# GFNet mixing and SwiGLU block: the order of loads and weight conversion in the first batch's head

## The chip, the cores and the metric

The kernel runs on one core of one Trainium2 chip. That core has TensorE (PE, with its weight loads PEld), VectorE (DVE), ScalarE (ACT), GpSimd (POOL) and SyncE (SP), and 16 DMA engines that serve the transfers which SP, ACT and POOL issue. The metric is the device time of one execution in microseconds. A profiled execution gives a span, which is a little shorter than the device time of the same execution.

## The reference

Eight batches of 3008 tokens with 256 channels are mixed along the tokens by a real Fourier transform, a multiplication with a complex filter and the inverse transform. Then every token passes a SwiGLU block with 1536 hidden channels. All values are float32 on the way in and out; the weights of the block come as 64-bit floats.

```python
X = np.fft.rfft(x, axis=1)
F = (filt_r + 1j * filt_i)[None, :, :]
y = np.fft.irfft(X * F, n=x.shape[1], axis=1)      # (8, 3008, 256)
x = y.reshape(8 * 3008, 256)
g = x @ w_gate                                     # (24064, 1536)
silu = g * (1.0 / (1.0 + np.exp(-g)))
out = (silu * (x @ w_val)) @ w_out                 # (24064, 256)
```

## The kernel before

**The whole.** The transform of length 3008 is split as 47 x 64. Batch by batch, a class `Spectral` carries it out in steps, and a class `Group` does the SwiGLU part. A batch has 8 chunks of tokens and the hidden layer has 3 parts, so 24 group steps make one batch. While TensorE works on the groups of batch b, the transform of batch b+1 is placed between them by a list of tokens (`SCHEDULE`). Only the first batch's transform has nothing to hide behind. It is the head of the program, and this case is about it. Every instruction of the head is issued by `pin`, which keeps the order in which the Python code issues it, so the order on each engine's queue is the order of the code. Each engine works its queue strictly in that order, and an instruction that waits holds everything behind it on that engine.

**The head's steps.** Four pieces of x (about 0.77 MB each) are loaded by `Spectral.load_x` into space that is lent by other tiles. `stage1_first(u)`, u = 0 to 7, is the first short transform: TensorE multiplies (L844), and the result is copied out of PSUM by ACT for one half of the channels and by DVE for the other (both L848). `turn(u)`, u = 0 to 11, transposes a unit on TensorE (L857), and ACT copies it (L861). `stage2a(u)`, u = 0 to 11, multiplies a unit by a table `tb` (L871). DVE then multiplies by the filter `f` in three operations of some 0.7 us (L880 with the filter's real part for both halves of the rows, L884 and L887 with the imaginary part), and POOL adds the two products (L326; for the last unit DVE does it). The real part is wanted in both halves of the rows, so `real_part(u)` copies it twice (L897): by POOL for every third unit (0, 3, 6, 9), else by ACT. `stage2b(u)`, four units behind, multiplies back by the table (L904), ACT copies the result (L912, the last one in two pieces L910), and it is written to DRAM (tensor `d`, L915). Units 0 to 7 are written from SP's queue, 8 to 11 from ACT's. `load_tables(i)`, i = 0 to 5, loads the table and the filter for two units: one transfer of 512 KB and four of 128 KB.

**Reload and stage 3.** `load_t4(0, i, part)` reloads the written result (`f<-d`), first the rows of units 0 to 7, then those of units 8 to 11. `stage3(0, step)` is the last transform for chunk 0 (L941). After it the first group begins (L1035). In front of stage 3 stand matmuls on zeros and on weights that compute nothing that is kept (`idle`, L578): five on zeros, one on the weights from slot A13 on and one on those from slot A01 on. The last two wait for those weights.

**The weights.** The 64-bit weights are turned into float32 on the chip, by halves of 262 KB. `weight_halves()` lists them: 8 hidden halves and 8 output halves for each of the 3 parts. `load_weights(i)` loads half i. `round_half(i)` converts it in nine small pieces: DVE takes the bits apart (L403, L406), ACT makes the power of two (L408, L411, L413, L415), DVE puts sign and low bits in (L418, L422), and POOL multiplies and adds up (L442, L443, then L329 or L326; L430 for an output half). Buffers for these are few: a half i uses the buffer of an earlier half, so its first operation on DVE waits until POOL has finished with that one. `combine_weights(g, i, j)` makes sums of converted halves for a pair of blocks: an add on DVE (L326 or L333), for some pairs a scaling on ACT (L464), a subtraction on POOL (L329), and an add on DVE for the first four pairs of part 0 and on POOL for the others.

**The ticks.** The class `Preparation` holds a timetable: to each tick belongs a list of such pieces. Half i starts four ticks after half i-1, half 8 (the first output half) eight ticks after half 7, and the pieces of a half stand at 0, 1, 2, 3, 4, 6, 7, 9 and 10 ticks from its start. The six pairs of part 0 are combined from tick 39 on. `tick(step, n)` issues the pieces of the next n ticks. With `hold=True` the pieces on POOL are kept back until `release()`. `finish(step)` issues all ticks that must stand before a group step. During the groups of batch 0, 20 ticks are issued per group step.

**The order in the code.** In the head, SP loads the four pieces of x, and then weight halves and tables in turn. Four ticks are issued at stage 1's last step, two after the first turns, two in each of the first ten units of stage 2a, and one in each of the last three rounds of stage 2b. `finish(0)` then issues the rest, 16 ticks, before stage 3.

Of the kernel before, what the change touches and what calls it, by code (L numbers as in the profile page):

```python
# [71 lines left out]
N_TWO = NS // NV  # L72
# [30 lines left out]
BLOCKS = (0, 1, 3, 2)  # L103
# [100 lines left out]
def kernel(  # L204
# [165 lines left out]
    def spot_of(i):  # L370

        spot = (i - N_EARLY) % 5
        return spot if i < N_LENT and spot < 3 else None
# [3 lines left out]
    def load_weights(i):  # L377
        if i in raws or i >= len(weights):
            return
        if i < N_EARLY:  # L380
            raws[i] = early_raw(i)
        elif spot_of(i) is not None:
            raws[i] = bits(4 * 7 * 128 + 512 * spot_of(i))
        else:
            raws[i] = rpool.tile([128, 2, 128, 2], U32, name=f"raw_{i}", tag="raw", bufs=2)
        pin(nc.sync.dma_start(out=raws[i], in_=weights[i][0]))
# [65 lines left out]
    def combine_weights(g, i, j):  # L452

        d = j - i
        wt_f = weights_of(0, 0, g).rearrange("p s z f -> p s (z f)")
        m = wt_f[:, SLOT[f"A{i}{j}"]]
        ui, uj, yi, yj = [wt_f[:, SLOT[f"{p}{q}"]] for p in "PQ" for q in (i, j)]
        if d == 1:
            pin(negated_sum(m, ui, uj))
        else:  # L460
            pin(add(nc.vector, m, ui, uj))
        yield
        if d > 1:
            pin(nc.scalar.mul(m, m, -1.0 / d))  # L464
        yield
        pin(sub(nc.gpsimd, wt_f[:, SLOT[f"B{i}{j}"]], yi, m))
        early = g == 0 and PAIRS_USED.index((i, j)) < 4
        pin(add(nc.vector if early else nc.gpsimd, wt_f[:, SLOT[f"E{i}{j}"]], yj, m))
# [10 lines left out]
    class Preparation:  # L479
# [3 lines left out]
        def __init__(self):  # L483
            self.at, self.held = 0, []

            self.ticks, self.need = {}, {}
            base, ready = [], {}

            def put(t, f, by, pool=False):
                self.ticks.setdefault(t, ([], []))[pool].append(f)  # L490
                self.need[by] = max(self.need.get(by, 0), t)

            for i, (_, (use, *at)) in enumerate(weights):
                hid, g = use == "hid", at[0] if use == "hid" else at[0] // JB
                by = ((0, 3, 6) if hid else (1, 4, 7))[g]
                b = base[-1] + (4 if i != 2 * len(BLOCKS) else 8) if i else 0
                if i >= N_EARLY:
                    same = [n for n in range(N_EARLY, i) if spot_of(n) == spot_of(i)]
                    k = 2 if spot_of(i) is None else 1
                    last = base[same[-k]] + 8 if same[k - 1:] else 0  # L500
                    b = max(b, last + 8)
                    put(max(last, b - 10), lambda i=i: load_weights(i), by)
                base.append(b)
                if hid and g == NG - 1:
                    ready.setdefault(NT, b)
                half = []

                def go(half=half, i=i):
                    if not half:
                        half.append(round_half(i))  # L510
                    next(half[0], None)

                for n, t in enumerate((0, 1, 2, 3, 4, 6, 7, 9, 10)):
                    put(b + t, go, by, n > 6)
                if hid and at[1:] == [BLOCKS[-1], 1]:
                    for n, pair in enumerate(PAIRS_USED):
                        c = combine_weights(g, *pair)
                        for t in range(3):

                            put(b + 11 + n + t, lambda c=c: next(c, None),  # L520
                                by if g or n < 4 else 1, t == 2)
            self.barriers = sorted((t, step) for step, t in ready.items())
            self.end = max(self.ticks)
# [27 lines left out]
    preparation = Preparation()  # L551
# [17 lines left out]
    def bank(name):  # L569
        return wps.tile([128, 512], FP32, name=f"w{name}", tag="w")  # L570
# [4 lines left out]
    def idle(t, banks, n):  # L575

        for ps in banks:
            pin(nc.tensor.matmul(out=ps[:, 0:n], lhsT=t[:, 0:128], rhs=t[:, 0:n],  # L578
                                 start=True, stop=True))
# [578 lines left out]
    def run(piece):  # L1158
        for _ in piece:
            pass  # L1160

    with tc.tile_pool(name="start", bufs=1) as spool0:
# [12 lines left out]
        n = 0  # L1175
# [9 lines left out]
        def early_raw(i):  # L1185
            if i >= 8:
# [7 lines left out]
        pin(nc.scalar.activation(out=one, in_=off_t, func=AF.Silu))  # L1194
        idle(zero, [bank("idle") for _ in range(3)], 512)
        pin(nc.sync.dma_start(out=wf_t, in_=wf_dram.ap()))
        load = [("x", 0), ("x", 1), ("x", 2), ("x", 3), ("w", 0), ("t", 0), ("w", 1), ("t", 1),
                ("w", 2), ("t", 2), ("w", 3), ("w", 4), ("t", 3), ("w", 5), ("w", 6), ("t", 4),
                ("w", 7), ("t", 5)]
        for what, i in load:  # L1200
            {"x": spec.load_x, "w": load_weights, "t": spec.load_tables}[what](i)
        for u in range(8):
            spec.stage1_first(u)
            if u == 7:
                preparation.tick(0, 4)
        for u in range(2):
            spec.turn(u)
        spec.real_part(0)
        preparation.tick(0, 2)
        lag = 4  # L1210
        for u in range(N_TWO + lag):
            if u < N_TWO:
                spec.turn(u + 2)
                step = spec.stage2a(u)
                next(step)
                if u % 3 == 1:
                    spec.real_part(u + 2)
                next(step)
                preparation.tick(0, 2 * (u < N_TWO - 2), hold=True)
                run(step)  # L1220
                preparation.release()
                if u % 3 != 2:
                    spec.real_part(u + 1)
            if u >= lag:
                if u == N_TWO:
                    idle(zero, [bank("idle")], 512)
                elif u > N_TWO:
                    preparation.tick(0)
                run(spec.stage2b(u - lag))
            if u == 6:  # L1230
                pin(nc.sync.dma_start(out=wi_t, in_=wi_dram.ap()))
                for i in range(8, N_EARLY):
                    load_weights(i)
            if u == N_TWO - 1:
                for i in range(2):
                    spec.load_t4(0, i, 0)
        for i in range(2):
            spec.load_t4(0, i, 1)
        for i in range(2):
            spec.load_t4(1, i)  # L1240
        preparation.finish(0)

        idle(zero, [bank("idle") for _ in range(5)], 512)
        for p in ("A13", "A01"):
# [85 lines left out]
    for b in range(B):  # L1330
# [35 lines left out]
        for step in range(NCHUNK * NG + (b == B - 1)):  # L1366
# [16 lines left out]
            for place, token in enumerate(SCHEDULE):  # L1383
# [8 lines left out]
                elif op[0] == "t":  # L1392
                    n = int(op[1])
# [20 lines left out]
                if b == 1 and step < 4 and op in FILTER_AT:  # L1414
                    n = FILTER_AT.index(op)
# [49 lines left out]
```

## Time and profile before

| what | value |
|---|---|
| median of 6 runs | 2828.01 us (2825.73 to 2829.28) |
| the profiled execution's own time | 2827.17 us |
| its span | 2825.4 us |
| last copy of stage 1 (L848, DVE) starts | 20.90 us |
| first matmul of stage 2a | 23.75 us |
| first L880 on DVE | 24.98 us |
| last unit's L880 on DVE | 60.38 us |
| last unit's write is issued | 65.83 us |
| first matmul of stage 3 | 74.33 us |
| first matmul of the first group | 78.76 us |

A line of the timeline is: start in us from the span's start, duration in us, engine, source line, operation, output <- inputs, shapes, count. In square brackets stands how long the engine had been idle before it and what released it. In the page's line of engines each has its busy time, that as a share of the span, and its instructions. In a line of windows, the stretch comes first and its length, then the busy time (and instructions) of PE, PEld, DVE, ACT and POOL, the clock granted to TensorE as a share of full speed, the share of time that the DMA engines were busy, and the GB/s that they moved.

### The profile page before, as it was taken

The page shows a single profiled execution, that of the slowest core. Times are in us where ns is not written, and L with a number is a line of the kernel's source. Part 1 is how long each engine was busy: PE and PEld are TensorE (multiplying, and loading weights), DVE is VectorE, ACT ScalarE, POOL GpSimd, SP SyncE. Part 2 cuts the span into 40 slices and gives each one's busy share as a digit, 9 for nine tenths or more (in the row PEclk, how much of TensorE's full clock was granted, in tenths as well). Part 3 has the DMA queues.
Part 4 walks back from the last instruction along what each step waited for, and adds up shares of the span by engine and source line. Part 5 has one row for each costly group of instructions (what it writes and reads, how often), then busy time and mean ns, then how long its engine had stood idle before and what let it go on. Part 6 is the DMA issues. An engine that isn't in the chain of part 4 may idle for free.

```text
span 2825.4 us, 48474 instructions
## 1 busy us (share of the span) xinstructions
PE 2782.6 (98%) x15432; PEld 2315.3 (82%) x15432; DVE 1991.4 (70%) x4555; ACT 1573.2 (56%) x4202; POOL 1578.1 (56%) x1683
## 2 busy tenths in 40 slices
PE   7999999999999999999999999999999999999998
PEld 5777878888888888788888888888888888888886
DVE  6898766767667766667766677667676767666666
ACT  6775445655555555555555555555555555555554
POOL 4886565465545655456654566444665455545544
PEclk9999999999999999999999999999999999999999
DMA  9687866877666775667666776667765677654543
GB/s 232 216 274 252 270 204 218 287 231 238 188 186 200 251 218 179 202 213 231 218 186 198 215 241 205 184 194 234 228 206 181 214 223 226 192 153 148 153 136 82
DMA packets 363373, 586.59 MB, mean 208 GB/s; under 512 B 198388, under 2 KB 246260, under 8 KB 363024
## 3 DMA queue, kind: packets, MB, share of 16 engines
q1 hardware_dynamic: 337922, 534.73, 60.5%
q10 hardware_dynamic: 23406, 45.43, 5.9%
q0 software_dynamic: 1792, 3.34, 0.5%
q8 instruction: 125, 2.05, 0.3%
q14 instruction: 128, 1.05, 0.1%
HBM read 467.87 MB, written 101.34 MB: 201 GB/s over the span
## 4 chain that ended last, share of the span: by engine, by line
PE 88%; POOL 3%; DVE 1%; issue 1%; DMA 1%; ACT 0%; SPq 0%; POOLq 0%; ACTq 0%; DVEq 0%
PE wa L1035 24%; PE wk L1035 16%; PE wA L1132 16%; PE we L1035 12%; PE wG L1132 8%; PE wF L1132 4%; PE pd L938 3%; PE wqa L690 2%; PE wqc L749 1%; PE wqb L761 1%; POOL out_dram L1117 1%; POOL h L329 1%; DMA lent<-later_tbl 0%; POOL h L326 0%; POOL y_t L326 0%
## 5 line engine op out<-in xcount | busy, mean ns | idle before, releaser
L1035 PE MATMUL wa<-y_t,wt_t 128*128 128x188 f32 x4464 | 879.7, 323 | 5.5 <-DVE wa L1057 1.6
L1035 PEld LDWEIGHTS wa<-y_t,wt_t 128*128 128x128 f32 x4464 | 747.4, 190 | 83.0 <-ACT wa L1061 10.8
L1035 PEld LDWEIGHTS wk<-y,wt_t 128*128 128x128 f32 x2976 | 494.6, 190 | 106.5 <-issue 33.8
L1035 PE MATMUL wk<-y,wt_t 128*128 128x188 f32 x2976 | 571.3, 325 | 0.1
L326 POOL TENSOR_TENSOR h<-h 128x376 f32<-128x376 f32 x190 | 183.5, 988 | 694.3 <-DVE h L1082 694.3
L329 POOL TENSOR_TENSOR h<-h 128x376 f32<-128x376 f32 x572 | 558.1, 998 | 15.4 <-DVE h L326 15.2
L1132 PE MATMUL wA<-h,wo_t 128*128 128x376 f32 x1532 | 551.1, 482 | 4.9 <-DVE o L326 4.8
L1035 PE MATMUL we<-y_t,wt_t 128*128 128x188 f32 x2232 | 432.5, 323 | 0.9 <-ACT we L1066 0.9
L329 POOL TENSOR_TENSOR D<-f,f 128x376 f32<-128x376 f32 x288 | 279.9, 986 | 253.6 <-ACT f L1050 252.0
L329 DVE TENSOR_TENSOR we<-we,m 128x376 f32<-128x376 f32 x576 | 319.7, 556 | 137.3 <-PE we L1035 72.9
L1035 PEld LDWEIGHTS we<-y_t,wt_t 128*128 128x128 f32 x2232 | 370.0, 190 | 1.8 <-ACT we L1066 1.4
L1132 PEld LDWEIGHTS wA<-h,wo_t 128*128 128x128 f32 x1532 | 274.9, 190 | 114.3 <-issue 7.6
L1070 ACT COPY m<-wa 128x376 f32<-128x376 f32 x576 | 272.7, 473 | 103.0 <-PE wa L1035 99.9
L333 DVE SCALAR_TENSOR_TENSOR y<-wk,c 128x376 f32<-128x376 f32 x480 | 244.8, 540 | 58.7 <-ACT c L1054 35.6
L1077 ACT ACTIVATE g<-wa 128x188 f32<-128x188 f32 x576 | 187.8, 326 | 163.7 <-PE wa L1035 153.1
L1077 ACT ACTIVATE u<-we 128x188 f32<-128x188 f32 x576 | 188.4, 328 | 159.1 <-DVE we L329 152.8
L1132 PE MATMUL wG<-h,wo_t 128*128 128x376 f32 x768 | 274.0, 479 | 0.0
L1054 ACT COPY c<-wk 128x376 f32<-128x376 f32 x288 | 136.4, 474 | 220.5 <-PE wk L1035 187.0
L1050 ACT ACTIVATE f<-wk 128x376 f32<-128x376 f32 x288 | 140.5, 488 | 170.0 <-PE wk L1035 121.0
L1066 ACT COPY we<-y 128x376 f32<-128x376 f32 x480 | 222.5, 480 | 21.3 <-DVE h L1082 14.0
L1082 DVE TENSOR_TENSOR h<-wa,g 128x188 f32<-128x188 f32 x576 | 199.2, 346 | 37.0 <-ACT g L1077 36.7
L1082 DVE TENSOR_TENSOR h<-we,u 128x188 f32<-128x188 f32 x576 | 197.9, 344 | 26.7 <-ACT u L1077 15.6
(163 smaller groups left out, 3517.9 us busy)
## 6 DMA issues: line engine op xcount, KB each, us to landing
wt_t<-w_all SPq DMA_DIRECT2D x174, 896.0 KB, 4.7
wt_t<-w_all SPq DMA_DIRECT2D x174, 768.0 KB, 4.3
lent<-filter SPq DMA_DIRECT2D x36, 1024.0 KB, 7.0
lent<-d SPq DMA_DIRECT2D x84, 256.0 KB, 4.0
d<-lent ACTq DMA_DIRECT2D x84, 256.0 KB, 3.8
d<-lent ACTq DMA_DIRECT2D x96, 192.0 KB, 3.2
lent<-raw SPq DMA_DIRECT2D x144, 128.0 KB, 2.1
t<-d SPq DMA_DIRECT2D x112, 128.0 KB, 4.5
```

The costliest lines, as they stand in the source:

```text
L326: return eng.tensor_tensor(out=dst, in0=a, in1=b, op=ALU.add)
L329: return eng.tensor_tensor(out=dst, in0=a, in1=b, op=ALU.subtract)
L333: return nc.vector.scalar_tensor_tensor(out=dst, in0=a, scalar=-1.0, in1=b, op0=ALU.mult, op1=ALU.subtract)
L938: pin(nc.tensor.matmul(out=rows, lhsT=self.t4[k, i][:, j, ts(cb, 128)], rhs=cols, start=j == 0, stop=True, skip_group_check=True))
L1035: pin(nc.tensor.matmul(out=ps[:, z], lhsT=self.wt[:, SLOT[p], z], rhs=rhs, start=start and z == 0, stop=True, skip_group_check=True))
L1050: pin(act.mul(self.small(f"f{i}", f"f{i}", 1), t[f"k{i}"], -1.0))
L1054: pin(act.copy(out=self.small(f"c{i}", f"c{i}", 1), in_=t[f"k{i}"]))
L1066: pin(act.copy(out=self.bank(f"e{at}"), in_=t[f"y{at}"]))
L1070: pin(act.copy(out=self.small(f"m{at}", "m", 4), in_=t[f"a{at}"]))
L1077: pin(act.activation(out=self.small(op, "g", 3, 1)[:, 0], in_=ps[:, 1], func=AF.Silu))
L1082: pin(v.tensor_tensor(out=dst, in0=ps[:, 0], in1=g, op=ALU.mult))
L1132: pin(nc.tensor.matmul(out=self.tiles[at], lhsT=wo_t[:, JB * q + i, WO[p], :], rhs=self.hs[i][:, HID[p]], start=start and i == 0, stop=Tru ...
```

## The change

The eight hidden halves of part 0 are no longer loaded between the tables. Halves 0 to 3 are loaded behind one piece of x each, halves 4 to 7 behind the last of those, and the six pieces of tables and filter behind all halves.

The ticks move with them. Four are issued after every second step of stage 1 (16 in all), nine after the first turns, and four in each of the first five units of stage 2a (two with POOL's pieces held back, two after the unit). With those 45, all eight hidden halves are converted, and their pairs are combined as far as `finish(0)` asks. No ticks are issued in the later units or in the rounds of stage 2b. Half 8 now starts 18 ticks after half 7 instead of 8, and with it all later halves start ten ticks later. Eleven ticks are issued behind `finish(0)`, which hold the rest of the last two pairs, half 8 and the beginning of halves 9 and 10. In the order of the changed program, all ten combining operations on DVE stand between the filter operations of units 3, 4 and 5; all operations of halves 0 to 4 on DVE stand before the first filter operation of unit 0, those of half 5 in part.

```diff
-                b = base[-1] + (4 if i != 2 * len(BLOCKS) else 8) if i else 0
+                b = base[-1] + (4 if i != 2 * len(BLOCKS) else 18) if i else 0
...
-        load = [("x", 0), ("x", 1), ("x", 2), ("x", 3), ("w", 0), ("t", 0), ("w", 1), ("t", 1),
-                ("w", 2), ("t", 2), ("w", 3), ("w", 4), ("t", 3), ("w", 5), ("w", 6), ("t", 4),
-                ("w", 7), ("t", 5)]
+        load = [("x", 0), ("w", 0), ("x", 1), ("w", 1), ("x", 2), ("w", 2), ("x", 3), ("w", 3)]
+        load += [("w", n) for n in range(4, 8)] + [("t", n) for n in range(6)]
         for what, i in load:
             {"x": spec.load_x, "w": load_weights, "t": spec.load_tables}[what](i)
         for u in range(8):
             spec.stage1_first(u)
-            if u == 7:
+            if u % 2:
                 preparation.tick(0, 4)
         for u in range(2):
             spec.turn(u)
+        preparation.tick(0, 9)
         spec.real_part(0)
-        preparation.tick(0, 2)
...
-                preparation.tick(0, 2 * (u < N_TWO - 2), hold=True)
+                preparation.tick(0, 2 * (u < 5), hold=True)
                 run(step)
                 preparation.release()
+                preparation.tick(0, 2 * (u < 5))
                 if u % 3 != 2:
                     spec.real_part(u + 1)
             if u >= lag:
                 if u == N_TWO:
                     idle(zero, [bank("idle")], 512)
-                elif u > N_TWO:
-                    preparation.tick(0)
                 run(spec.stage2b(u - lag))
...
         preparation.finish(0)
+        preparation.tick(0, 11)
```

## The prediction

> **What bounds the kernel now.** I read the page first: TensorE is busy 98% of the span, and the chain that ended last is TensorE's for 88% of it. From about 170 us on nothing in this change can move the time unless the beginning is shifted: what the head loses or wins is handed on one for one. (The page; its engine sums and the chain by engine.)
>
> ```profile
> PE 2782.6 (98%) x15432; PEld 2315.3 (82%) x15432; DVE 1991.4 (70%) x4555; ACT 1573.2 (56%) x4202; POOL 1578.1 (56%) x1683
> ...
> PE 88%; POOL 3%; DVE 1%; issue 1%; DMA 1%; ACT 0%; SPq 0%; POOLq 0%; ACTq 0%; DVEq 0%
> ```
>
> So I read the head by the timeline, engine by engine. DVE (start, duration, idle before it):
>
> ```profile
> 20.90 0.81 DVE L848 COPY lent<-wpa 128x384 f32<-128x384 f32 x1 [0.96 <-PE wpa L844]
> ...
> 24.98 0.69 DVE L880 TENSOR_TENSOR room<-wpb,y_t 128x512 f32<-128x512 f32 x1 [1.43 <-issue]
> 25.70 0.69 DVE L884 SCALAR_TENSOR_TENSOR y_t<-wpb,f 64x512 f32<-64x512 f32 x1
> ...
> 41.65 0.69 DVE L880 TENSOR_TENSOR room<-wpb,y_t 128x512 f32<-128x512 f32 x1
> ...
> 62.54 0.71 DVE L326 TENSOR_TENSOR room<-room,y_t 128x512 f32<-128x512 f32 x1
> ...
> 70.82 0.41 DVE L326 TENSOR_TENSOR wt_t<-wt_t 128x256 f32<-128x256 f32 x1
> ...
> 73.96 0.94 DVE L326 TENSOR_TENSOR wt_t<-wt_t 128x256 f32<-128x256 f32 x1
> ```
>
> Between the copies of stage 1 DVE idles 0.96 us each time; stage 2a's twelve units run from 24.98 to 63.25, 3.2 us a unit, although one unit is three operations 0.72 us apart (24.98, 25.70): the rest is conversion and waiting. The same combining add takes 0.41 or 0.94 us.
>
> POOL, ACT, SP and TensorE at the joints (timeline):
>
> ```profile
> 20.13 1.26 POOL L897 COPY y_t<-f 64x512 f32<-64x512 f32 x2 [19.68 <-PE wpa L844]
> ...
> 96.61 0.98 POOL L326 TENSOR_TENSOR y_t<-y 128x376 f32<-128x376 f32 x1 [0.89 <-PE we L1035]
> ```
> ```profile
> 63.63 7.42 SPq L596 DMA_DIRECT2D f<-d  x4
> ...
> 65.83 0.37 ACTq L915 DMA_DIRECT2D d<-x  x1
> ...
> 70.81 0.44 PEld L578 LDWEIGHTS widle<-wt_t 128*128 128x128 f32 x2 [2.91 <-POOL wt_t L326]
> ...
> 74.33 3.71 PE L941 MATMUL wpd<-wi_t,f 96*128 96x94 f32 x32
> ```
> ```profile
> 70.00:72.00 2.00, 1.16 (x2) 0.57 (x3) 2.00 (x5) 1.68 (x5) 1.85 (x4) 0.73 0.34 102
> 72.00:74.00 2.00, 2.00 (x3) 0.84 (x3) 2.00 (x4) 1.43 (x3) 1.64 (x3) 0.50 0.91 268
> ```
>
> Stage 3 starts at 74.33 because two things end together: the last weights (POOL, then four fill matmuls at clock 0.50, the last window rows) and the reload of stage 2b's last result, written at 65.83, whose reload SP can issue only at about 70.2.
>
> **The change, part by part.**
>
> *Loads.* No byte is added. The loads up to the last table and filter piece are 11.5 MB (x 3.08, eight halves 2.10, tables 3.15, filter 3.15); the windows of 10 us sum to 11.6 MB by 50 us, some 235 GB/s, so the order decides what is late. Ahead of filter piece 0 now stand seven more halves (1.84 MB, 7.8 us). It had landed by 20.1 (POOL L897 starts), so it lands at about 27.8. The last piece keeps its place (52 to 53 us). SP issues the same instructions, 0.39 us a half, inside its waits: free. The x pieces come 1 to 3 us later; stage 1's matmuls are 0.114 us apart without a gap (64 in 7.28 us) and take x piece 3 at 17.1; with three halves (0.79 MB, 3.3 us) ahead it comes at about 17 to 19. At most 1.5 us there, covered by the wait for filter piece 0.
>
> *Conversion in stage 1.* A half costs DVE 0.28+0.28+0.43+0.43 = 1.4 us, ACT 0.42+0.49+0.51+0.42 = 1.85. In the new order halves 0 to 4 are done on DVE before the first unit of stage 2a: 7 us in gaps of 8 x 0.96 and in the wait for the filter. Following ACT and DVE through that order, stage 1 ends at about 22 instead of 21.7: free.
>
> *Start of stage 2a.* POOL's copy of the filter, 27.7 to 28.95, then DVE: 28.95 instead of 24.98, **+4.0**.
>
> *Units 0 to 4.* Before: 24.98 to 41.65, 16.7 us. After: 15 operations x 0.72 = 10.8; what is left of halves 5, 6, 7, 3.4; the ten combining operations, which stood behind the stage at 69.2 to 76.8, 5.6 (their spacing there); and three new stalls that I find by walking the three queues: DVE's first operation of half 7 needs half 4's buffer, which POOL frees only behind unit 0's add (1.27) and the conversion, 2.3 us; unit 2 waits for ACT's filter copy (1.23) behind half 7's activations, 1.2; unit 4's copy stands on ACT behind a scaling (L464) that needs DVE's first combining add, 1.3. Behind each stall stand on DVE the rest of that unit and all later ones, on POOL their adds, on TensorE stage 2b. Together 24.6, **+7.9**. Bounds: no stalls and 0.34 a combining operation, 17.6; all at 0.94 and the stalls, 28.4. I take the middle, since the 0.94 rows are those beside a busy POOL, and POOL is busy about half of that time.
>
> *Units 5 to 11.* No conversion is left: 7 x 2.16 + 0.7 = 15.8 against 21.6 (41.65 to 63.25), **-5.8**. TensorE needs about 2.4 a unit but is two units ahead, and the data is there. Stage 2a ends at 69.3 instead of 63.25.
>
> *To the last write.* Before, 2.6 us from the add to the issue at 65.83, ACT being on a conversion; after, one pair of matmuls (1.1), ACT's two halves (0.63): 1.8, **-0.8**. The write took 4.3 us (65.83 to 70.2, SP's wait), behind four other transfers; after, the units come slower than the queue empties, and the writes issued into a quiet queue landed in 2.2 to 2.4: I take 2.4, **-1.9** (between 0 and -2.1).
>
> *Reload and start of stage 3.* Weights are long ready, so the fill matmuls on them no longer wait and run at full clock: 2b's end at 70.4 + 6 us of fill = 76.4, reload in by 76.8, no cold stretch: stage 3 at 76.8, **-0.9** against the old distance. Sum to here: +2.5 (74.33 to 76.8).
>
> *First group.* Ticks are ten later for half 8 on, and eleven more are run before stage 3: the same conversion is left, one tick less, but four combining operations of POOL (3.0) and one product (0.72) have left the group (87.32 to 93.0). POOL then reaches the row at 96.61 earlier and waits there for the same matmuls (it waited 0.89 already), so most is lost: between 0 and -3.7, I take **-0.5** since TensorE idles only some 0.5 us between 88.5 and 96.5.
>
> Sum: **+2.0 us**. The profiled execution took 2827.17 (span 2825.4 and 1.8 around it), 0.8 below the median of 2828.01: 2829.2 for it, **2830** against the median.
>
> *Two rules against the rows.* The clock rows: behind an idle time of 2.1 us before 70.84 the clock is halved (0.73 and 0.50 in the two windows, 3.4 us of half clock in all): 1.7 us lost. In the new order TensorE waits some 3 us for table 0; unit 0's matmuls (1.1) then take 2.2 and still end before POOL's copy does: nothing. In front of stage 3 a gap of 2 us or more would cost 1.7. The Trainium skill ("TensorE: Matmul & The Clock Gate", "Why this matters for your kernels") warns only of gaps over about 3 us: by it a gap of 2 to 3 us before stage 3 would be free. The 0.41 and 0.94 rows gave the combining operations 5.6. The skill's "GPSIMD Engine Reference" ("1. Specifications") has GpSimd share its SBUF interfaces with VectorE, in contention with instructions that have two SBUF inputs, as these have; read strictly, this speaks against moving them beside a busy POOL, and the sum would be higher by up to 3.8 us (an estimate: ten at 0.94).
>
> **Rivals.**
> 1. *The end of stage 2 meets a full queue (slower).* If the last write again takes 4.3 us and its reload 4.7 (the median of those reloads) instead of 2.7, the +1.9 and 2.0 come back: +5.9, 2834. For it: the reload of the first part is issued just before the last write. Against: in the old head they were issued 2 us apart (63.63, 65.83), in the new one by the order of the units some 4. It decides if it is over 9.4 us from that write's issue (71.1) to stage 3; before it was 8.5 (65.83 to 74.33).
> 2. *Stage 2 follows the loads (faster).* If DVE keeps up, unit 10 starts when the last filter piece has landed and been copied (53.4), the stage ends at 58.4, the last write goes out at 60.2, reload by 67.7, stage 3 cold (+1.7): -5.4, with POOL's relief -6: 2822. For it: DVE's 2.16 a unit fits the loads' 2.45. Against: the ten combining operations and the stalls above, all before unit 5. It decides if unit 5 starts by 46.
> 3. *Nothing moves.* Without the stalls but with everything else, unit 5 starts at 48.7, stage 2a ends at 64.5, stage 3 at 72: -2.3, with the first group -2.8, 2825.2. That is the low end of my own case.
>
> **How the numbers follow.** My case, -2.8 to +5, holds 0.71; rival 1 0.18, rival 2 0.11. 0.2% of this kernel, about what can be told from no change, is 5.7 us, so my case lies wholly within it; of rival 1 most lies just above, of rival 2 some two thirds below it. Faster 0.08, within 0.75, slower 0.17. The range 2824 to 2835 takes in my case, what lies below it by POOL's relief, and the lower half of rival 1.
>
> **What would show it.** Right: DVE's first L880 at about 29; a wait of DVE for POOL before unit 1 and for ACT's L897 before units 2 and 4; the fifth unit (counting from 0) at about 53; then 2.16 us a unit; last add at 69; stage 3 at 77, with the clock at 1.00; POOL's wait at the first y_t add longer by some 3 us. Wrong: a first L880 much later than 30 (halves slower than 235 GB/s), or unit 5 before 49, or stage 3's matmuls at clock 0.5.

## The result and the profile after

The changed kernel takes 2833.37 us in the median (2830.8 to 2839.85, 19 runs) against 2827.97 us (2825.45 to 2832.09, 39 runs) for the kernel before. The ratio is 1.0019, with a 95% interval from 1.0013 to 1.0025: 5.4 us slower. I had forecast 2830 in a range of 2824 to 2835, and no change that can be told as the likeliest. The direction of my sum was right and its size too small: +2.0 us by my steps, +5.4 measured.

The profiled execution has a span of 2831.5 us, 6.1 more than before. The page's line of engines and the line of the chain:

```profile
PE 2783.1 (98%) x15432; PEld 2317.5 (82%) x15432; DVE 1991.2 (70%) x4555; ACT 1573.2 (56%) x4202; POOL 1578.2 (56%) x1683
...
PE 88%; POOL 3%; DVE 1%; issue 1%; DMA 1%; ACT 0%; ACTq 0%; SPq 0%; POOLq 0%; DVEq 0%
```

No busy time has changed by more than 2.2 us, and the chain is TensorE's for 88% as before. The page can't show where the time went; the timelines of the head do. First VectorE, stage 2a:

```profile
28.83 0.67 DVE L880 TENSOR_TENSOR room<-wpb,y_t 128x512 f32<-128x512 f32 x1
...
34.56 0.29 DVE L403 TENSOR_SCALAR w<-wt_t 128x256 uint32<-128x256 uint32 x1 [2.52 <-POOL wt_t L326]
...
39.25 0.69 DVE L880 TENSOR_TENSOR room<-wpb,y_t 128x512 f32<-128x512 f32 x1 [1.23 <-ACT y_t L897]
...
44.55 0.71 DVE L326 TENSOR_TENSOR wt_t<-wt_t 128x256 f32<-128x256 f32 x1
45.18 1.49 DVE L333 SCALAR_TENSOR_TENSOR wt_t<-wt_t 128x256 f32<-128x256 f32 x1
46.89 0.69 DVE L880 TENSOR_TENSOR room<-wpb,y_t 128x512 f32<-128x512 f32 x1 [0.22 <-ACT y_t L897]
...
48.33 0.43 DVE L326 TENSOR_TENSOR wt_t<-wt_t 128x256 f32<-128x256 f32 x1
48.68 0.83 DVE L333 SCALAR_TENSOR_TENSOR wt_t<-wt_t 128x256 f32<-128x256 f32 x1
...
50.25 1.83 DVE L326 TENSOR_TENSOR wt_t<-wt_t 128x256 f32<-128x256 f32 x2
52.01 0.95 DVE L333 SCALAR_TENSOR_TENSOR wt_t<-wt_t 128x256 f32<-128x256 f32 x1
52.88 2.69 DVE L326 TENSOR_TENSOR wt_t<-wt_t 128x256 f32<-128x256 f32 x3
55.49 0.68 DVE L880 TENSOR_TENSOR room<-wpb,y_t 128x512 f32<-128x512 f32 x1
...
70.60 1.14 DVE L326 TENSOR_TENSOR room<-room,y_t 128x512 f32<-128x512 f32 x1
```

The first filter operation stands at 28.83 (before 24.98), unit 5's at 55.49 (41.65), the last add ends at 71.74 (63.25). Between units 3 and 5 stand the ten combining operations on the weights: 1.49 us for one, 1.83 for two, 2.69 for three; only one of them, at 48.33, takes 0.43. GpSimd was at work beside them, at the last of them with the same kind of operation, as its timeline shows:

```profile
44.92 1.46 POOL L326 TENSOR_TENSOR room<-room,y_t 128x512 f32<-128x512 f32 x1
...
47.87 1.36 POOL L897 COPY y_t<-f 64x512 f32<-64x512 f32 x2
50.37 1.44 POOL L326 TENSOR_TENSOR room<-room,y_t 128x512 f32<-128x512 f32 x1 [1.14 <-DVE y_t L887]
51.77 3.52 POOL L329 TENSOR_TENSOR wt_t<-wt_t 128x256 f32<-128x256 f32 x4
```

The queues and TensorE, up to the first group:

```profile
70.45 7.80 SPq L596 DMA_DIRECT2D f<-d  x4
...
73.64 0.37 ACTq L915 DMA_DIRECT2D d<-x  x1
```
```profile
77.05 1.88 PE L578 MATMUL widle<-wt_t 128*128 128x512 f32 x4
79.93 3.78 PE L941 MATMUL wpd<-wi_t,f 96*128 96x94 f32 x32 [1.00 <-issue]
...
84.44 0.80 PE L1035 MATMUL wk<-y,wt_t 128*128 128x188 f32 x4
```

The last write is issued at 73.64 (65.83), between SP's reloads of the first part (from 70.45) and of the second (77.45). Stage 3 starts at 79.93 (74.33) at full clock, and the first group's first matmul at 84.44 (78.76), 5.68 us later. Some of this comes back in the first group. TensorE's second pair of L1132 waits for converted output weights; before, and then in the changed kernel with the first pair ahead of it:

```profile
105.69 0.90 PE L1132 MATMUL wF<-h,wo_t 128*128 128x376 f32 x2 [1.81 <-POOL wo_t L430]
```
```profile
108.49 0.80 PE L1132 MATMUL wF<-h,wo_t 128*128 128x376 f32 x2
110.68 0.90 PE L1132 MATMUL wF<-h,wo_t 128*128 128x376 f32 x2 [1.40 <-POOL wo_t L430]
```

It stands at 110.68 against 105.69, 4.99 us later. After that the head is over, and the offset is handed on. The same instructions of VectorE, ScalarE and GpSimd, matched in both traces, are 4.9 us later up to 330 us, 5.65 from 350 us on and 6.9 from 545 us on. Whether those two steps belong to the change is not shown. At 339 and at 545 us work waits for transfers; the trace with the loads alone changed has steps of -0.5 and +2.2 there, and run 1 below, which loads in the changed order too, has none above 0.1 at either place.

### The profile page after: what moved, and what is told of

It is laid out like the page before. It is cut to its first block, busy times and chain, and to the rows that moved or that the text cites. A ratio compares the mean times of both kernels' runs of the same rounds, so it can differ in the third digit from the quotient of the medians.

```text
span 2831.5 us, 48483 instructions
## 1 busy us (share of the span) xinstructions
PE 2783.1 (98%) x15432; PEld 2317.5 (82%) x15432; DVE 1991.2 (70%) x4555; ACT 1573.2 (56%) x4202; POOL 1578.2 (56%) x1683
## 4 chain that ended last, share of the span: by engine, by line
PE 88%; POOL 3%; DVE 1%; issue 1%; DMA 1%; ACT 0%; ACTq 0%; SPq 0%; POOLq 0%; DVEq 0%
PE wa L1035 24%; PE wk L1035 16%; PE wA L1132 16%; PE we L1035 12%; PE wG L1132 8%; PE wF L1132 4%; PE pd L938 3%; PE wqa L690 2%; PE wqc L749 1%; PE wqb L761 1%; POOL out_dram L1117 1%; POOL h L329 1%; DMA wt_t<-w_all 0%; DMA lent<-later_tbl 0%; POOL y_t L326 0%
## 5 line engine op out<-in xcount | busy, mean ns | idle before, releaser
L1132 PE MATMUL wA<-h,wo_t 128*128 128x376 f32 x1532 | 551.1, 482 | 4.3 <-DVE o L326 4.2
L1132 PEld LDWEIGHTS wA<-h,wo_t 128*128 128x128 f32 x1532 | 274.9, 190 | 113.7 <-issue 8.2
L1132 PE MATMUL wG<-h,wo_t 128*128 128x376 f32 x768 | 274.0, 479 | 0.0
L1082 DVE TENSOR_TENSOR h<-we,u 128x188 f32<-128x188 f32 x576 | 198.0, 344 | 26.7 <-ACT u L1077 15.6
```

What stands on the lines that cost most here:

```text
L1082: pin(v.tensor_tensor(out=dst, in0=ps[:, 0], in1=g, op=ALU.mult))
L1132: pin(nc.tensor.matmul(out=self.tiles[at], lhsT=wo_t[:, JB * q + i, WO[p], :], rhs=self.hs[i][:, HID[p]], start=start and i == 0, stop=Tru ...
```

## The experiments

Two theories stood against each other at the start. Mine: VectorE's queue through stage 2a sets the end of the head; it starts late, has waits in it, and above all ten combining operations that GpSimd makes slow. The rival: the end is set by transfers (late filter pieces; the last write and its reload in a full queue) and by TensorE's clock at stage 3, so that shortening VectorE's queue brings nothing.

In the profiled executions with all halves loaded ahead, the first L880 starts between 28.6 and 31.0 us, and once at 37.2, although the order of the loads is the same. In runs 2 and 6 GpSimd's copy of the filter waits for the transfer until 29.41 and 29.72 us, in run 12 it runs at 27.00 without a wait; the 37.2 has another cause (run 1). So I read stage 2a as the distance from the first L880 to the start of DVE's last add, which takes that difference out. In kernels with added lines the numbers of the lines are 3 or 6 higher (L883 or L886 is L880). Each ratio is to the runs of the kernel before in the same rounds, whose medians were 2827.17 to 2828.23; differences of medians between rounds hold that much uncertainty.

| kernel | first L880 | distance to the last add | stage 3 | first group | median us | ratio to before (95%) |
|---|---|---|---|---|---|---|
| before | 24.98 | 37.56 | 74.33 | 78.76 | 2827.97 | 1 |
| changed | 28.83 | 41.77 | 79.93 | 84.44 | 2833.37 | 1.0019 (1.0013 to 1.0025) |
| loads alone | 30.71 | 37.99 | 79.00 | 83.43 | 2831.49 | 1.0015 (1.0006 to 1.0024) |
| combining behind | 37.23 | 33.02 | 79.79 | 87.69 | 2826.29 | 0.9998 (0.9990 to 1.0006) |
| third buffer | 29.00 | 40.37 | 78.56 | 85.02 | 2834.18 | 1.0026 (1.0017 to 1.0035) |
| third buffer, fill | 31.02 | 40.38 | 81.28 | 85.71 | 2832.79 | 1.0017 (1.0008 to 1.0026) |
| GpSimd later, fill | 30.08 | 39.64 | 79.60 | 84.03 | 2830.60 | 1.0010 (1.0001 to 1.0018) |
| both | 30.08 | 31.66 | 72.06 | 79.71 | 2825.57 | 0.9993 (0.9985 to 1.0002) |
| both, fill | 30.42 | 31.80 | 72.70 | 77.50 | 2823.62 | 0.9989 (0.9980 to 0.9997) |
| tables nearer | 26.64 | 35.13 | 72.06 | 76.70 | 2825.02 | 0.9995 (0.9986 to 1.0004) |
| reload split | 29.67 | 31.62 | 69.87 | 76.67 | 2824.26 | 0.9990 (0.9981 to 0.9999) |
| split, GpSimd later | 28.63 | 31.62 | 68.83 | 73.37 | 2823.15 | 0.9987 (0.9978 to 0.9996) |

(Two more, the reload last and the group without its early steps, stand with their own numbers below.)

**1. The combining operations moved back.**

```diff
-                preparation.tick(0, 2 * (u < 5), hold=True)
+                preparation.tick(0, 2 * (u < 4), hold=True)
...
-                preparation.tick(0, 2 * (u < 5))
+                preparation.tick(0, 2 * (u < 3))
```

> The changed kernel, with the ten combining operations of the first weights put back behind stage 2a; order of the loads and conversion as changed. Theory (VectorE's stream sets the end of stage 2a, and the combining operations, 8.6 us there beside a busy GpSimd, are its largest new part): unit 5 starts at 46 to 47 instead of 55.5, stage 2a ends at 62 to 63 instead of 71.7, stage 3 starts at 71 to 73 instead of 79.9, time 7 to 8 us below the changed kernel, 2825 to 2827. Rival A (loads and reload set stage 3): unit 5 early, but stage 3 not before 76, time 2 to 4 us below the changed kernel. Rival B (now the weights come last, as before): stage 3 at 74.3, time as the kernel before.

Measured: 2826.29, 7.1 below the changed kernel (5.9 by the ratios). The profiled execution is a poor sample of these runs: it took 2836.21. Its clock was 0.50 from 12.36 us for 23.9 us, and stage 1 ran at that clock (32 matmuls in 7.03 us, 3.78 in the changed kernel), so that the first L880 stands at 37.23, 8.4 later:

```profile
23.07 7.03 PE L844 MATMUL wpa<-wf_t,x 94*128 94x96 f32 x32
```

Counted from the first L880, unit 5 comes after 17.9 us (26.7), the last add after 33.02 (41.77). The theory held: 8.75 us left VectorE's queue ahead of the last add, and the time follows it for four fifths (two thirds by the ratios). Rival A and rival B both fell, since with stage 3 at 42.6 from the first L880 it is 8.5 nearer to it than in the changed kernel. The ten operations, now behind the stage, show the contention within one trace: up to 73.77, with GpSimd idle, they take 0.41 to 0.43, and from the moment that its subtractions begin 0.94 or 0.95:

```profile
73.77 0.43 DVE L326 TENSOR_TENSOR wt_t<-wt_t 128x256 f32<-128x256 f32 x1 [1.82 <-ACT wt_t L464]
74.11 0.95 DVE L333 SCALAR_TENSOR_TENSOR wt_t<-wt_t 128x256 f32<-128x256 f32 x1
```
```profile
73.81 4.43 POOL L329 TENSOR_TENSOR wt_t<-wt_t 128x256 f32<-128x256 f32 x5 [4.35 <-ACT wt_t L464]
```

**2. The loads alone.** The kernel before with the new list `load`, and no tick moved.

> The kernel before with the new order of the loads alone; every conversion step stays where it was. Theory (the late filter shifts VectorE's stream, which has no slack): first L880 at 28.8 instead of 24.98, stage 2a ends at 67 instead of 63.25, stage 3 at 78, time 4 us above the kernel before, 2832. Rival (before, stage 2a also waited for halves and tables that now are there, so it catches up): stage 2a ends at 64, time within 1 us of the kernel before.

Measured: 2831.49, 4.0 above the kernel before in the same rounds (2827.49). The wait for the filter is the start's whole delay, and the distance stays (37.99 for 37.56):

```profile
30.71 0.69 DVE L880 TENSOR_TENSOR room<-wpb,y_t 128x512 f32<-128x512 f32 x1 [6.53 <-POOL y_t L897]
```

The theory held. As long as the conversion keeps its place in stage 2a, late tables are paid in full there: the stage ends 6.2 us later (69.41 for 63.25), and stage 3 starts 4.7 later, 1.5 of it having come back on the way.

**3. A buffer of their own for halves 6 and 7.** The two use free space behind x instead of the two shared buffers.

```diff
+        elif i in (6, 7):
+            w = extra_w[i - 6]
         else:
             w = rpool.tile([128, 2, 128], FP32, name=f"w_{i}", tag="w", bufs=2)
```

> The changed kernel, with room of their own for the mantissas of halves 6 and 7, so that half 7 no longer needs half 4's buffer. Theory (VectorE's waits add up): the wait of 2.52 us for GpSimd before L403 at 34.6 is gone, unit 5 starts at 53 instead of 55.5, stage 3 at 77.4 instead of 79.9, time 2.5 us below the changed kernel, 2831. Rival (the next wait, for ScalarE's filter copy, takes it up): unit 5 at 55, time within 1 us of the changed kernel.

Measured: 2834.18, no gain. DVE's wait of 2.52 us is gone, but the distance fell by 1.4 us only. The loss is at unit 1 already, which starts 1.45 us nearer to the first L880: the operation that had waited (L403, here L406) took 0.29 us behind its wait and takes 1.36 now, beside GpSimd's add of unit 0. Unit 2's wait for ScalarE is still there and smaller (0.81 for 1.23).

```profile
32.13 1.36 DVE L406 TENSOR_SCALAR x<-wt_t 128x256 uint32<-128x256 uint32 x1
```
```profile
31.89 1.45 POOL L326 TENSOR_TENSOR room<-room,y_t 128x512 f32<-128x512 f32 x1 [2.96 <-issue]
```

And that 1.4 was lost again at stage 3 (TensorE's timeline):

```profile
75.83 1.88 PE L581 MATMUL widle<-wt_t 128*128 128x512 f32 x4
78.56 4.90 PE L944 MATMUL wpd<-wi_t,f 96*128 96x94 f32 x32 [0.86 <-issue]
```

The idle time before stage 3 is no longer than in the changed kernel (0.86 for 1.00), and yet the clock granted is 0.50 from 80.99 on for 6.83 us, and the 32 matmuls take 4.90 instead of 3.78. So the theory was half right (unit 5 comes 1.4 us nearer, not 2.5), and the rival had the right time for a wrong reason.

**4. Both edits together.**

> The changed kernel with both edits: combining operations behind stage 2a, and room of their own for halves 6 and 7. Theory (both are parts of one stream): unit 5 at 43.5 to 44.5, stage 2a ends at 60 to 61, stage 3 at 70 to 71, time 9 to 10 us below the changed kernel, 2823 to 2825, below the kernel before. Rival (without them the loads set the pace: the last piece of the filter lands at 52 to 53 and two units stand behind it): stage 2a ends at 62, no earlier than with the combining operations moved alone, time the same as that one.

Measured: 2825.57, 7.8 below the changed kernel. Unit 5 at 46.59 with the first L880 at 30.08, distance 31.66: 10.1 us less than in the changed kernel, as the two edits add up. The loads did not hold it up. Unit 5 comes later than the theory had it (46.59 for 43.5 to 44.5); 1.25 of that is the later start, and the slow operation of run 3 stands here too (1.37). And TensorE now runs out of fill, and the windows show the clock at 0.50 (column before the last two):

```profile
72.06 6.10 PE L944 MATMUL wpd<-wi_t,f 96*128 96x94 f32 x32 [2.44 <-issue]
```
```profile
75.00:76.00 1.00, 1.00 (x6) 1.00 (x6) 0.53 (x3) 0.94 (x4) 0.73 (x1) 0.50 1.12 297
```

**5. Both, with three more fill matmuls** (`idle` with eight banks instead of five).

> Both edits (combining operations behind stage 2a, room of their own for halves 6 and 7), and three more fill matmuls (0.86 us each) in front of stage 3, so that TensorE does not wait 2.4 us for the reload there. Theory (there the clock was 0.50 from 73.4 to 80.0 us behind that wait, which cost 3.3 us): stage 3 at about 72.2 with the clock at 1.00, its 32 matmuls in 3.7 to 3.8 us instead of 6.10, time 3.3 us below both edits without fill, 2822. Rival (the clock falls whatever stands in front, for instance by the pauses in stage 2): 0.50 again at stage 3, time as both edits or up to 0.2 us more.

Measured: 2823.62, 2 us below the run without fill by the medians (expected 3.3; the intervals overlap), and below the kernel before (0.9989, 0.9980 to 0.9997). Stage 3 is at full clock, and the first group starts at 77.50 instead of 79.71:

```profile
72.70 3.78 PE L944 MATMUL wpd<-wi_t,f 96*128 96x94 f32 x32
```

**6. The buffers with two more fill matmuls.**

> The changed kernel with room of their own for halves 6 and 7, and two more fill matmuls. Theory (that edit alone brought stage 3 from 79.9 to 78.6, and the clock of 0.50 from 80.95 to 87.7 took 3.35 us, more than it had won): stage 3 at 78.7 to 79.0 with the clock at 1.00, time 1 us below the changed kernel, 2832. Rival (the clock falls whatever stands in front): time as with that edit alone, 2834.

Measured: 2832.79, 1.4 below the buffers alone. The 32 matmuls take 3.71 us at full clock. The intervals overlap, so only the trace shows the cause; the time agrees with the theory.

**7. Tables behind four halves instead of eight.**

```diff
+        load = [("x", 0), ("w", 0), ("x", 1), ("w", 1), ("x", 2), ("w", 2), ("x", 3), ("w", 3),
+                ("t", 0), ("w", 4), ("w", 5), ("t", 1), ("w", 6), ("w", 7)]
+        load += [("t", n) for n in range(2, 6)]
...
-        preparation.tick(0, 9)
+        preparation.tick(0, 4)
```

The 19 ticks left up to the combining operations are spread over units 0 to 4; the buffers and the fill are as in 5.

> As both edits with three more fill matmuls, but table and filter piece 0 loaded behind four halves instead of eight, piece 1 behind six, and the conversion steps of halves 5 to 7 that stood ahead of stage 2a spread over its first five units. Theory (the late filter costs the start, 4 us by my step): first L880 at 25 to 26 instead of 29 to 30, stage 2a ends at 59 to 61, stage 3 at 69 to 71, time 1 to 3 us below both edits with fill, 2819 to 2821. Rival (the start is no bound: VectorE has the same conversion to do either way, and the filter's last piece lands at 52 to 53): unit 5 and the end of stage 2a as with both edits and fill, time within 1 us of it.

Measured: 2825.02, 1.4 above 5 and within its noise. The rival held. VectorE starts 3.78 us earlier than in 5 (26.64 for 30.42), and the last add comes 0.45 us earlier (61.77 for 62.22):

```profile
26.64 0.68 DVE L883 TENSOR_TENSOR room<-wpb,y_t 128x512 f32<-128x512 f32 x1
```

Whether VectorE converts while it waits for the filter or after is nearly the same. What counts here is the sum of its work and waits until the last add: from unit 5 on it runs at 2.16 us a unit in both.

**8. The reload behind the last write.** The two transfers for the rows of units 8 to 11 go first, then those for units 0 to 7.

> The changed kernel with the two reloads of the first part moved behind the last write (the two of the second part go first). It tells what that write and its reload cost when no reload of the first part is beside them. Theory (the write took 3.7 us because it met those two reloads): last write issued at 73.6, landed by 76.0, SP's next issue at 76.1 instead of 77.4; but four reloads then follow it, stage 3 at 80.5 to 82, time 1 to 2 us above the changed kernel, 2834.5 to 2835.5. Rival (a write takes 3.7 us there anyway): SP's issue at 77.4, stage 3 at 82 to 83.5, time 2 to 3.5 us above.

Measured: 2839.03 (ratio 1.0043, 1.0029 to 1.0056), 5.7 above the changed kernel. The queues:

```profile
74.40 0.37 ACTq L915 DMA_DIRECT2D d<-x  x1
...
76.58 2.04 SPq L596 DMA_DIRECT2D f<-d  x4
```

The write alone: 2.18 us to SP's next issue, against 3.81 in the changed kernel (73.64 to 77.45). So the theory on the write held. The other traces agree: the nearer the first part's reload stands ahead of the last write, the longer until SP's next issue (1.3 us ahead and 4.92 in run 5, 2.2 and 4.43 before, 3.2 and 3.81 in the changed kernel, 5.7 and 2.26 in run 11). I had put the four reloads behind it too low: stage 3 came at 83.14, at half clock for 10.2 us.

**9. GpSimd's four subtractions later.** VectorE's combining operations stay between units 3 and 5. The steps ahead of stage 3 keep their total.

```diff
+        if not early:
+            pin(sub(nc.gpsimd, wt_f[:, SLOT[f"B{i}{j}"]], yi, m))
         pin(add(nc.vector if early else nc.gpsimd, wt_f[:, SLOT[f"E{i}{j}"]], yj, m))
+        if early:
+            yield
+            pin(sub(nc.gpsimd, wt_f[:, SLOT[f"B{i}{j}"]], yi, m))
...
+                        if not g and n < 4:
+                            put(b + 18 + n, lambda c=c: next(c, None), by, True)
...
-        preparation.tick(0, 11)
+        preparation.tick(0, 6)
```

> The changed kernel, with the four GpSimd subtractions that stand beside VectorE's combining operations (3.52 us at 51.77) put behind stage 2a, and two more fill matmuls so that stage 3 meets no long wait. VectorE's ten combining operations stay between units 3 and 5. Theory (an operation with two SBUF inputs takes 0.42 us beside an idle GpSimd and 0.8 to 0.95 beside a busy one): the six operations from 50.25 to 55.5 take 2 to 2.5 us instead of 5.2, unit 5 starts 2.5 to 3 us earlier against the first L880, time 2 to 3 us below the changed kernel, 2830.5 to 2831.5. Rival (they take 0.85 us each for another reason, such as their own tiles or the transfers): unit 5 at the same distance from the first L880, 26.7 us, time as changed.

Measured: 2830.60, 2.8 below the changed kernel. VectorE, and GpSimd beside it:

```profile
51.52 1.83 DVE L326 TENSOR_TENSOR wt_t<-wt_t 128x256 f32<-128x256 f32 x2
53.27 0.41 DVE L333 SCALAR_TENSOR_TENSOR wt_t<-wt_t 128x256 f32<-128x256 f32 x1
53.61 1.08 DVE L326 TENSOR_TENSOR wt_t<-wt_t 128x256 f32<-128x256 f32 x3
54.62 0.68 DVE L886 TENSOR_TENSOR room<-wpb,y_t 128x512 f32<-128x512 f32 x1
```
```profile
51.63 1.43 POOL L326 TENSOR_TENSOR room<-room,y_t 128x512 f32<-128x512 f32 x1 [1.14 <-DVE y_t L893]
```

While GpSimd adds (51.63 to 53.06), two operations still take 1.83; once it is idle, four take 1.4. In the changed kernel the same four, at 52.01 and 52.88, took 3.6. Unit 5 comes 24.5 us after the first L880 instead of 26.7. The six take 3.2 us instead of 5.3; the theory had 2 to 2.5, because it did not count the add beside the first two. Its cause held, and this is the contention measured by itself: the same operations on the same tiles, with GpSimd's subtractions away.

**10. Without the eleven steps ahead of stage 3.**

```diff
         preparation.finish(0)
-        preparation.tick(0, 11)
```

> The changed kernel without the eleven conversion steps ahead of stage 3, which then run in the first group. It measures my term for the first group. Theory (what is run ahead there is work that the group hides, so nothing comes back): first group's first matmul at 84.4 as before, time within 1 us of the changed kernel. Rival (my step: the work moved out of the group is worth 0.5 to 3.7 us): time 0.5 to 3.7 us above the changed kernel, 2834 to 2837.

Measured: 2841.08 (1.0043, 1.0030 to 1.0056), 7.7 above. Both expectations fell. Stage 3 meets half clock (6.83 us from 81.8 on), which puts the first group 2.9 us later (87.33 for 84.44; 0.2 of it is stage 3's later start). Then TensorE waits in the first group for converted output weights:

```profile
114.60 0.90 PE L1132 MATMUL wF<-h,wo_t 128*128 128x376 f32 x2 [3.07 <-POOL wo_t L430]
118.85 1.62 PE L1132 MATMUL wF<-h,wo_t 128*128 128x376 f32 x2 [3.35 <-POOL wo_t L430]
```

In the changed kernel the first of these pairs did not wait (108.49) and the second waited 1.40 (110.68); they stand 6.1 and 8.2 us later here. A second stretch of half clock (6.83 us from 115.9 on) lies over the second. The steps are not spare work that the group hides. The run does not measure my term for the group, though: it leaves more conversion in the group than the kernel before had there, and part of its loss is the clock's.

**11. The reload cut at row 48**, so that its first part needs only units 0 to 5 and goes out two units earlier; on top of both edits, with one more fill matmul.

```diff
-                r = (slice(0, 64), slice(64, NK))[part]
+                r = (slice(0, 48), slice(48, NK))[part]
...
-            queue = nc.scalar if self.b or u >= 8 else nc.sync
+            queue = nc.scalar if self.b or u >= 6 else nc.sync
...
-            if u == N_TWO - 1:
+            if u == 10:
```

> Both edits and one more fill matmul, and the reload cut at row 48 instead of 64: its first part needs units 0 to 5 alone and goes out two units earlier, the writes of units 6 and 7 go to ScalarE's queue. Theory (the last write meets no reload any more, as the run with the reload last showed, 2.2 us): SP issues the second part 2.2 to 2.6 us behind the last write instead of 4.8, stage 3 at 70 to 71 instead of 72.7, time 2 us below both edits with three fill matmuls, 2821 to 2822. Rival A (the weights' last combining operations or the fill set stage 3): stage 3 at 72. Rival B (a second part of 48 rows lands later by what the split wins): stage 3 at 72 to 73, time as both edits with fill.

Measured: 2824.26, no better than 5. The last write goes out at 64.39, SP issues the second part at 66.65, 2.3 us later, and stage 3 starts at 69.87, 2.8 earlier than in 5. But the next wait took its place:

```profile
69.87 3.71 PE L944 MATMUL wpd<-wi_t,f 96*128 96x94 f32 x32
...
76.67 1.62 PE L1038 MATMUL wk<-y,wt_t 128*128 128x188 f32 x4 [2.20 <-DVE y L326]
```

The first group waits for y, which DVE and ACT deliver late because their combining operations and the conversion behind these end late (the ten stand from 61.90 to 70.8), and the clock falls for 6.83 us. This is near rival A: what set the limit was the weights, though on the way to the group and not to stage 3.

**12. The same, with GpSimd's four subtractions later** as in 9.

> As the run with the reload cut at row 48, and GpSimd's four subtractions behind its other combining operations. There stage 3 started at 69.87, but the first group's first matmul waited until 76.67 for VectorE and ScalarE, which still converted behind ten combining operations slowed by GpSimd (61.9 to 70.8), and the clock then fell to 0.50 for 6.83 us (3.4 lost). Theory (contention with GpSimd is what is late): the ten end by 68 to 69 instead of 70.8, that first matmul comes at 74.3 to 75 with the clock at 1.00, time 3 to 5 us below that run, 2819 to 2821. Rival (GpSimd's other operations stand beside them then, and the conversion steps are as late): first matmul at 76 to 77, half clock, time 2823 to 2825.

Measured: 2823.15 (0.9987, 0.9978 to 0.9996). VectorE's ten operations and the first matmuls:

```profile
64.72 0.42 DVE L333 SCALAR_TENSOR_TENSOR wt_t<-wt_t 128x256 f32<-128x256 f32 x1
65.05 2.15 DVE L326 TENSOR_TENSOR wt_t<-wt_t 128x256 f32<-128x256 f32 x3
```
```profile
68.83 3.71 PE L950 MATMUL wpd<-wi_t,f 96*128 96x94 f32 x32
...
73.37 0.90 PE L1044 MATMUL wk<-y,wt_t 128*128 128x188 f32 x4
```

The wait for y and the half clock are gone in the trace: the first group starts 3.3 us earlier than in 11 and 5.4 earlier than before, as the theory has it. The median moved by 1.1 us only (2.2 against the kernel before of each one's own rounds, 0.9 by the ratios), and its interval overlaps with 5 and 11. It is below both the kernel before and the changed one, and can't be told from 5. Why the timed executions win less than the profiled one is open; the first L880, late or early by 2.4 us between traces, is one candidate that no run isolates.

## Why the prediction was right and where it was wrong

From the first L880 to the first group, step by step, as the prediction has them:

| step | predicted | measured |
|---|---|---|
| start of stage 2a | +4.0 | +3.85 (28.83 for 24.98) |
| units 0 to 4 | +7.9 | +9.99 (26.66 for 16.67) |
| units 5 to 11 | -5.8 | -5.35 (16.25 for 21.60) |
| to the last write's issue | -0.8 | -0.68 (1.90 for 2.58) |
| landing of the last write | -1.9 | -0.62 (3.81 for 4.43) |
| reload, start of stage 3 | -0.9 | -1.59 (2.48 for 4.07) |
| stage 3 | +2.5 | +5.60 (79.93 for 74.33) |
| first group | -0.5 | -0.7 (+5.68 to +4.99) |
| total | +2.0 | +4.9 to the end of the head; +5.4 in the medians |

The sum missed 3.1 us up to stage 3: 2.1 in units 0 to 4, 1.3 in the landing, 0.5 in units 5 to 11, less 0.7 in the reload.

**Right.** The order of the parts and the signs of all of them. The first L880 came 0.12 us from its forecast (such a close hit is luck, as other traces with these loads have it from 28.6 to 31.0), the waits for POOL (2.52, I had 2.3) and for ScalarE before unit 2 (1.23, I had 1.2) stand where the walk along the queues put them, and units 5 to 11 run at 2.16 us each; the 0.5 there is the last add, which takes 1.14 us beside GpSimd instead of 0.71. That no clock would be lost at stage 3 was right (1.00 from 60 to 86 us), and so was that GpSimd would wait longer at the first add on y_t (3.45 for 0.89) and little of its relief be won.

**What was luck.** The time lies in the range, but above the +5 that I gave as the top of my own case: the range holds it because it takes in the lower half of rival 1, whose condition failed. And that top was too low by my own bounds: with 28.4 us for units 0 to 4, 3.8 more than I took, the sum is +5.8. The change is 0.19%, just inside the 0.2% that I had called no change, and the runs tell it from none.

**Mis-sized: the ten combining operations, in "units 0 to 4".** I took 5.6 us, their spacing in the old place, and called 0.94 each an upper bound. They took 8.6: 2.1 from 44.55, 1.2 from 48.33, 5.3 from 50.25. The reason I had given for the middle, "POOL is busy about half of that time", was the error: POOL works beside all ten of them, with its adds, conversion steps, a copy and the subtractions of the same pairs, which follow the same ticks; only one (48.33, beside the copy) kept its 0.43. Run 9 shows that it is GpSimd, and run 1 that it is these operations that lengthen stage 2a. Unit 4's wait was smaller than I had put it (0.22 for 1.3), because the slow operation ahead of it covered it; that gave 1.1 back.

The Trainium skill ("GPSIMD Engine Reference", "1. Specifications") names a cause: GpSimd shares its SBUF interfaces with VectorE, in contention with instructions of two SBUF inputs. The runs agree in the main (0.41 alone, 0.94 or 0.95 beside GpSimd; L880, whose other input is in PSUM, keeps 0.67 to 0.69). The prediction had named up to 3.8 us for a strict reading of this rule and added nothing.

**Mis-sized: the landing of the last write.** I took the quiet queue's 2.4 us and had 3.81. Rival 1 named the mechanism, and its condition failed (6.3 us from the last write to stage 3, not over 9.4), but a part of its price was paid: the reload of the first part goes out as soon as unit 7's write has landed, 3.2 us ahead of the last write (70.45 and 73.64), and meets it. Run 8 gives the write alone 2.18. The reload that follows came 0.7 us shorter than I had it, which makes up half.

**Rivals 2 and 3.** Both needed stage 2a without the combining operations or without the waits. Run 4, which takes both out, brings unit 5 at 46.6 with a first L880 at 30.1, so rival 2's pace was there in the changed kernel's order of loads; the ticks kept it from it.

**What the change is worth, then.** By the ratios, times 2828: loads alone +4.2; with the ticks as written +5.4; with the combining operations behind stage 2a -0.6; with the buffers and three fill matmuls on top -3.1. So in these runs the new order of loads comes out below the kernel before, clear of its interval, only with the combining operations out of stage 2a, the buffers and the longer fill. Whether the old order of loads would gain as much from the same edits, no run shows.

## What to carry to other kernels

Conversion that is run ahead gained here only where the engine was waiting; moved into a stage that the same engine bounds, it was paid there. Before moving elementwise work with two SBUF inputs, look at what GpSimd does in the new place: beside it the same operation took more than twice the time. And when one wait before a TensorE stage is shortened, see that the fill in front still reaches to the new start, or the clock takes part of the gain (run 4: 6.10 us for the 32 matmuls instead of 3.78).

## What the runs showed of the hardware that I had not expected

- Stretches of half clock come in multiples of 3.41 us: 3.41, 6.83, 10.24, 13.65 and 23.89 in the traces (those at a trace's end aside). The Trainium skill ("TensorE: Matmul & The Clock Gate", "What's actually happening") has a free-running window of 3413 ns, which agrees. Its rule against gaps over about 3 us ("Why this matters for your kernels") does not: an idle time of 0.86 us before stage 3 was followed by 6.83 us at half clock (run 3), while 1.00 us in the changed kernel was followed by none. What decides between these two was not found. Nor what ends a stretch: in run 1, 64 matmuls of stage 1 run without a gap from 16.24 to 30.10 us, and the clock stays at 0.50.
- GpSimd is slowed by the contention too: its subtraction of 128x256 took 0.73 us alone and 0.88 (3.52 for four) beside VectorE's combining operations.
- A conversion step of VectorE with one SBUF input (L403, 0.28 us alone) took 0.70 at 28.21 beside GpSimd's copy in the changed kernel, and 1.36 beside its add in run 3. So it is not two inputs alone that are hit. (The page of GpSimd cited above also names VectorE instructions in a 2-port mode; whether L403 is one, no run here shows.)
- With the loads in the same order, GpSimd's copy of the first filter piece ran at 27.00 us without a wait in run 12 and had to wait for the transfer until 29.72 in run 6.
